# Four-fold streaming of the mixing products, and a mode-major layout of their input

## The chip, the cores and the metric

The kernel runs on one core of a Trainium2 chip. The metric is the device time of one execution in microseconds (us), lower is better. The core has five engines that run at the same time and meet through semaphores: TensorE (PE: matmuls, and PEld, its weight loads), VectorE (DVE), ScalarE (ACT), GpSimd (POOL) and SyncE (SP). SP and POOL issue DMAs here. Matmuls write to PSUM, which has eight banks of 512 float32 columns; ACT and DVE copy results from there to SBUF, the on-chip memory of 128 partitions.

## What is computed

Two operations in a row, on x of shape (8, 5696, 128) and h of shape (5696, 128):

```python
Yf = rfft(x, n=2*S, axis=1) * rfft(h, n=2*S, axis=0)
u0 = irfft(Yf, n=2*S, axis=1)[:, :S, :]          # long convolution

X = rfft(u0, axis=1)                             # 64 lowest modes are mixed
Yr = einsum('bmd,mde->bme', Xr, w_r) - einsum('bmd,mde->bme', Xi, w_i)
Yi = einsum('bmd,mde->bme', Xr, w_i) + einsum('bmd,mde->bme', Xi, w_r)
y = irfft(Yr + 1j*Yi, n=S, axis=1)
u = u0 + y
out = u + relu(u @ w_ch)
```

The mixing is the part that the change touches: for each of 64 modes m, two 128 x 128 weight matrices act on the real and imaginary parts of 8 batches, that is on 16 columns of 128 numbers.

## The kernel before, in words

All transforms are matmuls with constant matrices; operands in SBUF are float16, sums in PSUM float32. A recorder (class Recorder, lines 21 to 121) takes the instructions in the order in which the Python code issues them, keeps that order on each engine, and puts in the waits that the reads and writes of tiles and banks ask for. Nothing is reordered by a scheduler: the program order of each engine is the order of the code.

The batches go in four pairs (g_ = 0 to 3). For each pair, `a_tile` (line 462) makes a first transform (PE products F,Xin; copies to As by ACT and DVE), and `tick` (line 667) runs through the frequencies in steps: `second` (line 608, products As,M), `products` (line 628, the DVE multiplies by the filter, tiles Xs, U and Hs), the first part of the way back (products U,Wc, copies to Zs or Zt, DMA to the scratch tensor zscr), and at line 727 the products G,Zs, which add up the lowest modes of the pair in bank 7 (`MB`). Some matmuls (`keep`, line 575; WARM, line 433) compute nothing that is used.

At the end of each pair two copies bring the modes from bank 7 to the tile XT: line 757 (real and imaginary parts, 256 elements a partition, ACT) and line 759 (the negated imaginary part, 128 elements, ACT; for the last pair the DVE). Copies by two different engines from one bank go one after the other. XT holds 8 x 192 float16 a partition (`XTW` = 192 a batch): before, a batch is a row, with 64 values of -Xi, 64 of Xr and 64 of Xi.

After the last pair comes the stretch that the change is about, in this order on PE (lines 834 to 855):
- `u_z(0, 0, 0, True)`: sixteen products S4a,ZT0a and S4b,ZT0b of 89 columns for the first output tile;
- `mix(0, 16)`, eight more S4 products, `mix(16, 32)`, eight more, `mix(32, 64)`, eight more. `mix` issues for each mode two products with a weight load each (W as weights, XT as the moving operand, 16 columns), adding up in bank 6 (modes 0 to 31) or bank 7 (modes 32 to 63);
- copies of bank 6 (ACT, line 841) and bank 7 (DVE) to the tile Y; then eight transposes of Y by PE (line 846), eight S4 products, and copies of the transposed banks to the tile C (line 851: ACT for the first, DVE for the second half); the DVE then mirrors the second half of the table IBs (`reflect`, line 853).

Then comes the output loop (lines 910 to 928). `u_tile` (line 809) adds to each S4 sum the product of C with the table IBs (`u_c`, line 802, 356 columns) and copies the sum to UT (ACT or DVE); `o_tile` (line 863) multiplies UT by w_ch (products WI,UT), applies relu on ACT (line 893), adds on the DVE (line 894) and writes out by DMA from SP. The S4 products read ZT0 to ZT4, which SP loads from zscr (`load_zt`, line 527): ZT0 to ZT3 before and ZT4 right after the last pair, and each again when its turn is over. The sums take turns in four places of two banks each (`LSLOT`, line 777), so a place must have been copied to UT before PE fills it again.

The part of the code before that issues the products:

```python
for ri, first_col in ((0, M + m), (1, m)):
    mm(pv(6 + m // 32, m % 32 * 2 * B, [[1, 2 * B]]), w_sb[:, (ri * M + m) * D:(ri * M + m + 1) * D],
       bass.AP(xt, first_col, [[B * XTW, P], [M, 2], [XTW, B]]), ri == 0, ri == 1, WT + XTT, [bank(6 + m // 32)])
```

An access pattern is written as pairs of a step and a count: the 16 columns here are two parts (step 64) of eight batches (step 192).

## Time and profile before

| | |
|---|---|
| median of three runs | 379.84 us (379.36 to 381.79) |
| the profiled execution, time | 378.84 us |
| the profiled execution, span from first to last instruction | 377.0 us |
| mean granted clock of TensorE | 0.99 |
| mixing products (XT,W) | 128, from 256.6 to 261.0 us |
| copies to XT on ACT, 256 elements | 4, 386 ns each |
| copies to XT on ACT, 128 elements | 3, 273 ns each |
| copy to XT on the DVE, 128 elements | 1, 290 ns |
| copies to Y | ACT 586 ns, DVE 692 ns |
| products C with IBs, 356 columns | 128, from 263.4 to 363.7 us |

How to read the profile: "busy" is time in which an engine has an instruction in hand; for PE, matmuls overlap, so a busy PE may still stream few columns. In the row of 40 slices a digit is a share in tenths, 9 being 90% or more; PEclk is the share of TensorE's full clock that was granted. A line of a group or of the timeline names the source line, the engine, the operation, the tile written <- tiles read, the shape and the count; in brackets stand the idle time before it and what ended it. The chain that ended last is followed back from the last instruction: each piece is a start, a duration, an engine and a line, and "issue" is time without a visible cause. The times of one profiled execution hold for that execution; each engine's clock time is counted from the start of its span.

### The profile page before, as it was taken

How to read it: one execution, taken by the hardware profiler on the slowest of the kernel's cores; microseconds unless marked ns; L12 is line 12 of the kernel's file. 1: busy time of each engine (PE TensorE's matmuls, PEld its weight loads, DVE VectorE, ACT ScalarE, POOL GpSimd, SP SyncE). 2: the span in 40 equal slices, each digit the busy share in tenths (PEclk: the TensorE clock that was granted, in tenths of full speed). 3: DMA queues.
4: the chain of work that ended last, by engine and by line, in shares of the span. 5: the costliest groups of instructions: out<-in, count | busy, mean ns of one | idle time of the engine just before them, and what ended most of it. 6: DMA issues, size and time to landing. Idle time of an engine off the chain costs nothing.

```text
span 377.0 us, 12488 instructions
## 1 busy us (share of the span) xinstructions
PE 359.5 (95%) x5370; PEld 279.1 (74%) x5370; DVE 294.8 (78%) x336; ACT 314.1 (83%) x495; POOL 75.0 (20%) x117
## 2 busy tenths in 40 slices
PE   7889899999999999999999999999999999999994
PEld 7878766666866666866667766668899889988873
DVE  3649889988998999989998988873437767756666
ACT  8469789998989997999997999995457776788885
POOL 8713011200743220842311301133000000000000
PEclk9999999999999999999999999998899999999999
DMA  7999979979899997999994999999999999999878
GB/s 146 207 285 369 250 163 238 234 201 269 92 148 206 249 246 206 109 137 218 260 269 136 115 345 359 372 358 384 375 394 351 355 416 407 422 408 379 327 292 330
DMA packets 87048, 103.94 MB, mean 276 GB/s; under 512 B 22730, under 2 KB 72522, under 8 KB 83438
## 3 DMA queue, kind: packets, MB, share of 16 engines
q1 hardware_dynamic: 64610, 81.33, 61.4%
q0 software_dynamic: 22384, 21.83, 35.3%
q8 instruction: 42, 0.69, 0.8%
q14 instruction: 12, 0.10, 0.1%
HBM read 70.61 MB, written 51.12 MB: 323 GB/s over the span
## 4 chain that ended last, share of the span: by engine, by line
PE 72%; ACT 10%; DMA 6%; DVE 5%; POOL 3%; issue 3%; DVEq 0%; POOLq 0%
PE ps L323 72%; ACT As L313 7%; DMA Xr<-in_x_dram 4%; DVE As L317 2%; DMA Xt<-in_x_dram 2%; POOL Xr L320 2%; DVE U L622 1%; ACT Zs L311 1%; ACT Xs L311 1%; POOL Hin L320 1%; DVE Xin L365 1%; DVE Hs L315 1%; ACT R L893 1%; ACT Zt L311 1%; DVE U L655 0%
## 5 line engine op out<-in xcount | busy, mean ns | idle before, releaser
L655 DVE TENSOR_TENSOR U<-Xs,Hs 128x2048 f16<-128x2048 f16 (+1 forms) x73 | 86.6, 1192 | 13.9 <-ACT Xs L311 13.0
L323 PE MATMUL ps<-U,Wc 128*128 128x512 f16 (+1 forms) x368 | 94.1, 376 | 1.4 <-DVE U L622 1.4
L311 ACT CAST Xs<-ps 128x1024 f16<-128x1024 f32 (+1 forms) x77 | 74.8, 979 | 10.0 <-PE ps L323 6.9
L311 ACT CAST Zs<-ps 128x512 f16<-128x512 f32 (+1 forms) x132 | 69.2, 594 | 1.7 <-PE ps L323 1.7
L894 DVE TENSOR_TENSOR O<-ps,R 128x512 f32<-128x512 f32 x81 | 52.3, 684 | 20.1 <-ACT R L893 11.2
L317 DVE TENSOR_SCALAR As<-ps 128x720 f16<-128x720 f32 (+1 forms) x67 | 55.6, 880 | 5.7 <-PE ps L323 4.0
L893 ACT ACTIVATE R<-ps 128x512 f32<-128x512 f32 (+1 forms) x92 | 50.5, 591 | 8.5 <-PE ps L323 8.4
L323 PE MATMUL ps<-F,Xin 128*128 128x180 f16 x512 | 52.4, 250 | 3.8 <-DVE Xin L365 2.4
L323 PE MATMUL ps<-As,M 64*128 64x128 f16 (+2 forms) x1488 | 51.9, 215 | 1.2 <-ACT As L313 1.2
L323 PEld LDWEIGHTS ps<-F,Xin 128*128 128x128 f16 x512 | 44.5, 155 | 11.2 <-DVE As L317 3.0
L313 ACT ACTIVATE As<-ps 128x720 f16<-128x720 f32 (+1 forms) x65 | 45.8, 768 | 7.2 <-PE ps L323 6.7
L323 PE MATMUL ps<-WI,UT 128*128 128x256 f16 x360 | 51.0, 278 | 0.5 <-ACT UT L311 0.4
L323 PEld LDWEIGHTS ps<-U,Wc 128*128 128x128 f16 x368 | 28.7, 97 | 30.3 <-ACT Zs L311 3.7
L311 ACT CAST UT<-ps 128x712 f16<-128x712 f32 x46 | 34.5, 752 | 19.5 <-PE ps L323 18.6
L323 PEld LDWEIGHTS ps<-As,M 64*128 64x128 f16 x1488 | 41.6, 94 | 7.5 <-ACT As L313 1.7
L323 PEld LDWEIGHTS ps<-WI,UT 128*128 128x128 f16 x360 | 39.0, 152 | 3.4 <-issue 1.8
L323 PE MATMUL ps<-IBs,C 128*128 128x356 f16 x128 | 40.5, 326 | 0.1
L320 POOL DMA_DIRECT2D Xt<-in_x_dram x40 | 21.5, 541 | 79.1 <-PE ps L323 78.6
L323 PEld LDWEIGHTS ps<-G,Zs 128*128 128x128 f16 x512 | 26.1, 96 | 14.5 <-ACT Zs L311 2.0
L655 DVE TENSOR_TENSOR U<-ps,Hs 128x2048 f16<-128x2048 f32 x15 | 34.2, 2283 | 0.0
L323 PE MATMUL ps<-G,Zs 128*128 128x128 f16 (+2 forms) x512 | 32.3, 192 | 0.1
L311 ACT CAST Zt<-ps 128x512 f16<-128x512 f32 x52 | 28.5, 624 | 0.3 <-PE ps L323 0.3
(74 smaller groups left out, 487.3 us busy)
## 6 DMA issues: line engine op xcount, KB each, us to landing
out_dram<-O SPq DMA_DIRECT2D x39, 512.0 KB, 7.4
zscr<-Zs SPq DMA_DIRECT2D x62, 256.0 KB, 6.3
zscr<-Zt SPq DMA_DIRECT2D x26, 256.0 KB, 6.0
Xt<-in_x_dram POOLq DMA_DIRECT2D x20, 320.0 KB, 6.8
W<-wscr SPq DMA_DIRECT2D x4, 1024.0 KB, 6.7
ZT0a<-zscr SPq DMA_DIRECT2D x4, 1024.0 KB, 7.8
M<-cM POOLq DMA_DIRECT2D x5, 720.0 KB, 17.4
ZT1a<-zscr SPq DMA_DIRECT2D x3, 1024.0 KB, 8.5
```

The costliest lines, as they stand in the source:

```text
L311: R.add(e, lambda h_: h_.copy(dst, src), reads, writes, after=after)
L313: R.add(e, lambda h_: h_.activation(dst, src, COPY, scale=scale), reads, writes, after=after)
L315: R.add(e, lambda h_: h_.tensor_copy(dst, src), reads, writes, after=after)
L317: R.add(e, lambda h_: h_.tensor_scalar_mul(dst, src, scale), reads, writes, after=after)
L320: R.add(eng, lambda h_: h_.dma_start(dst, src), reads, writes, ring=ring, after=after)
L323: R.add("tensor", lambda h_: h_.matmul(o, l, r, start=st, stop=sp), reads, writes)
L365: R.add("vector", lambda e: e.tensor_copy(bass.AP(x_sb, i * XN * XS, [[XW, NQ], [XS, XN], [1, D]]), src), list(toks) + XZ, [("xin", i)])
L622: R.add("vector", lambda e: e.tensor_tensor(bass.AP(u_s[0], b * 512 + d0, [[2048, P], [1024, 2], [D, n], [1, d1 - d0]]), bass.AP(s_[0], s_ ...
L655: R.add("vector", lambda e: e.tensor_tensor(uv, src, hv, MULT), bk + [("h", t, 0), ("h", t, 1, 0), ("h", t, 1, J)], [("u", i)])
L893: R.add("scalar", lambda e: e.activation(rv, src_r, RELU), bk, [("r", i % NR)], after=once(("r", i % NR), G_ALL + XTT + [("y", 0), ("y", 1 ...
L894: R.add("vector", lambda e: e.tensor_tensor(ov, src_u, rv, ADD), bk + [("r", i % NR)], [key + (h_,)], after=once(key, old))
```

## The change

XT gets another layout, and the products another moving operand; nothing else differs.

In XT, 24 neighbours now belong to one mode: 8 of -Xi, 8 of Xr, 8 of Xi, the batches side by side. The copies at lines 757 and 759 write to it in pairs of neighbours (the two batches of a pair) with a step of 24 from mode to mode, and read bank 7 with a step of 128 inside such a pair. Their number, engines and elements are as before.

A product's 16 columns are now neighbours, and its moving operand repeats them n times (a step of 0, n = 4, or fewer for the last three modes of a bank), so that it has 64 columns. The 48 further columns are written to the places of the next three modes in the bank. The first product of a mode starts the sum anew (ri == 0), so the next mode's products overwrite what was put there; the values that stay are those of before.

```diff
-        evac(bass.AP(xt, 2 * g_ * XTW + M, [[B * XTW, P], [XTW, 2], [1, P]]), pv(MB, 0, [[P, 2], [1, P]]),
+        evac(bass.AP(xt, 2 * g_ + B, [[B * XTW, P], [B, 2], [3 * B, M], [1, 2]]), pv(MB, 0, [[M, 2], [1, M], [P, 2]]),
              [bank(MB)], [("xt", g_)], 1.0 / 64, eng="scalar", after=[("ag", k) for k in range(NS + 2 * XN, NK)])
-        evac(bass.AP(xt, 2 * g_ * XTW, [[B * XTW, P], [XTW, 2], [1, M]]), pv(MB, M, [[P, 2], [1, M]]),
+        evac(bass.AP(xt, 2 * g_, [[B * XTW, P], [3 * B, M], [1, 2]]), pv(MB, M, [[1, M], [P, 2]]),
              [bank(MB)], [("xtn", g_)], -1.0 / 64, eng="vector" if g_ + 1 == NP else "scalar", after=[("ag", k) for k in range(NS + 2 * XN, NK)])
...
+    MC = 4
+
     def mix(m0, m1):
         for m in range(m0, m1):
-            for ri, first_col in ((0, M + m), (1, m)):
-                mm(pv(6 + m // 32, m % 32 * 2 * B, [[1, 2 * B]]), w_sb[:, (ri * M + m) * D:(ri * M + m + 1) * D],
-                   bass.AP(xt, first_col, [[B * XTW, P], [M, 2], [XTW, B]]), ri == 0, ri == 1, WT + XTT, [bank(6 + m // 32)])
+            for ri, first_col in ((0, (3 * m + 1) * B), (1, 3 * m * B)):
+                n = min(MC, 32 - m % 32)
+                mm(pv(6 + m // 32, m % 32 * 2 * B, [[1, 2 * B * n]]), w_sb[:, (ri * M + m) * D:(ri * M + m + 1) * D],
+                   bass.AP(xt, first_col, [[B * XTW, P], [0, n], [1, 2 * B]]), ri == 0, ri == 1, WT + XTT, [bank(6 + m // 32)])
```

## The prediction

> **What bounds the kernel now.** I read the page first, then the chain that ended last in order of time, then TensorE's (PE's) granted clock stage by stage, then the instructions around the mixing. Lines of the page:

> ```profile
> span 377.0 us, 12488 instructions
> PE 359.5 (95%) x5370; PEld 279.1 (74%) x5370; DVE 294.8 (78%) x336; ACT 314.1 (83%) x495; POOL 75.0 (20%) x117
> ...
> PEclk9999999999999999999999999998899999999999
> DMA  7999979979899997999994999999999999999878
> ...
> PE 72%; ACT 10%; DMA 6%; DVE 5%; POOL 3%; issue 3%; DVEq 0%; POOLq 0%
> ```

> PE is the bound, and its clock is granted in full except in two of forty slices. The chain, around and behind those slices:

> ```profile
> 262.05 1.05 PE ps L846 x8
> 263.09 90.94 PE ps L323 x1292
> 354.03 0.08 issue
> 354.11 10.27 PE ps L323 x130
> ```

> From 263 to 364 us the end is set by PE alone, matmul behind matmul, with 0.08 us of "issue" between. What PE gains shortly before 263 us should therefore arrive at the end. I then cut the dip into the stretches in which the clock is constant (about 3.41 us each). Columns: busy us and count of each engine, then PEclk, DMA share, GB/s.

> ```profile
> core 0: us, PE busy (x) PEld busy (x) DVE busy (x) ACT busy (x) POOL busy (x), PEclk, DMA share, GB/s
> 24.80:28.21 3.41, 1.68 (x21) 1.44 (x18) 1.77 (x3) 0.47 (x1) 0.90 (x2) 1.00 1.01 387
> 256.91:260.32 3.41, 3.41 (x114) 3.41 (x111) 1.36 (x1) 2.39 (x2) 0.62 (x1) 1.00 1.06 362
> 260.32:263.73 3.41, 3.18 (x56) 2.92 (x53) 1.29 (x3) 0.60 (x1) 0.00 (x0) 0.50 1.05 397
> 263.73:267.15 3.42, 3.42 (x25) 2.33 (x24) 1.49 (x2) 1.41 (x2) 0.00 (x0) 0.50 1.03 356
> ```

> For two stretches, 6.8 us, the clock is exactly half. The stretch ahead of them is full of instructions (PE and weight loads busy 3.41 of 3.41 us), but almost all of these are mixing products. The same stretch, products (tile XT) alone:

> ```profile
> 256.91:260.32 3.41, 3.06 (x98) 2.90 (x95) 0.00 (x0) 0.00 (x0) 1.00 1.06 362
> ```

> The timeline gives the rates (start, us, engine, line, operands, count):

> ```profile
> 256.58 1.11 PE L323 MATMUL ps<-XT,W 128*128 128x16 f16 x32 [0.20 <-issue]
> 257.54 0.20 PE L323 MATMUL ps<-S4a,ZT0a 128*128 128x89 f16 x1
> ...
> 257.87 1.11 PE L323 MATMUL ps<-XT,W 128*128 128x16 f16 x32
> 258.82 0.20 PE L323 MATMUL ps<-S4a,ZT0a 128*128 128x89 f16 x1
> ...
> 259.16 2.05 PE L323 MATMUL ps<-XT,W 128*128 128x16 f16 x64
> 261.05 0.24 PE L323 MATMUL ps<-S4a,ZT0a 128*128 128x89 f16 x1
> ...
> 262.05 1.05 PE L846 MATMUL ps<-Id,Y 128*128 128x128 f16 x8 [0.23 <-issue]
> 262.89 0.28 PE L323 MATMUL ps<-S4a,ZT0a 128*128 128x89 f16 x1
> ...
> 263.49 2.28 PE L323 MATMUL ps<-IBs,C 128*128 128x356 f16 x7
> 265.56 0.28 PE L323 MATMUL ps<-S4a,ZT0a 128*128 128x89 f16 x1
> ...
> 267.25 0.20 PE L323 MATMUL ps<-S4a,ZT1a 128*128 128x89 f16 x1
> ...
> 268.08 0.31 PE L323 MATMUL ps<-IBs,C 128*128 128x356 f16 x1
> 268.24 0.20 PE L323 MATMUL ps<-S4a,ZT1a 128*128 128x89 f16 x1
> ```

> At the full clock a 16-column product takes 29.7 ns (32 from 257.87 to 258.82), an 89-column one 41 ns (8 from 257.54 to 257.87), a 356-column one 160 ns (268.08 to 268.24). In the dip: a 128-column transpose 105 ns (8 from 262.05 to 262.89), 89 columns 75 ns (8 from 262.89 to 263.49), 356 columns 296 ns (7 from 263.49 to 265.56). So the longer forms go at half rate. At 160 ns for 356 columns the array takes 2.2 columns a ns, some 7,600 in 3.41 us. The stretch before the dip streamed 98 x 16 + 16 x 89 = 2,990, or 39% (98 counts a few begun earlier). The stretch at 24.80 us, with the clock kept, has 21 matmuls of 180 columns, some of them begun earlier too, 3,780 columns or 50% at most, though PE was busy in only half of it. What the clock follows, as far as these rows show, is columns streamed and not time occupied.

> **The change part by part.**

> *Products, four times as wide.* The 128 products stay 128, each with its weight load; 116 have 64 columns, the last three of each bank (modes 29 to 31 and 61 to 63, two parts each) 48, 32 and 16. Price at the full clock: no row has 64 columns over all 128 rows of the array, so the ends are the 16-column product (29.7 ns, +0) and an 89-column matmul, 42 ns (sixteen of them and one 356 lie between 267.25 and 268.08: (0.83 - 0.16) / 16), which is +12 ns, or 1.6 us over 128. Between, the line through 89 columns (42 ns) and 356 (160 ns) falls 0.44 ns a column and gives 42 - 25 x 0.44 = 31 ns at 64. I take that, as both its rows are of this kind of stream: +1.3 ns, over 126 +0.16 us, all on the path, as the DVE's copy of Y waits for the last product. [...]

> *Copies into XT with pairs of neighbours.* Same count and elements (ACT 4 of 256 and 3 of 128, DVE one of 128), but written in pairs and read with a stride. No row has this form exactly; the nearest are the As copies (L313, L317), written in pieces of four with a strided source:

> ```profile
> L317 DVE TENSOR_SCALAR As<-ps 128x720 f16<-128x720 f32 x63 | 53.7, 902 | 5.7 <-PE ps L323 4.0
> L313 ACT ACTIVATE As<-ps 128x720 f16<-128x720 f32 x61 | 44.2, 785 | 7.2 <-PE ps L323 6.7
> L313 ACT ACTIVATE XT<-ps 128x256 f16<-128x256 f32 x4 | 1.5, 386 | 1.6 <-PE ps L323 1.6
> L317 DVE TENSOR_SCALAR XT<-ps 128x128 f16<-128x128 f32 x1 | 0.3, 290 | 2.6 <-ACT XT L313 2.6
> ```

> ACT: (785 - 386) / 464 = 0.86 ns an element; DVE: (902 - 290) / 592 = 1.03. Both are one step per element whatever the pieces, so I take 0. Upper end: the element part doubles, 256 x 0.86 + 128 x 1.03 = 0.35 us for the last pair, which lies on the path (PE idles 0.20 us for it at 256.58). At the three earlier group ends the two ACT copies (384 elements) would add 0.33 us each where ACT carries the chain: 1.3 us in all. Below nothing is excluded, since no row shows fewer than one step per element.

> *The dip.* In the stretch before it the products would stream 98 x 64, with the 16 others some 7,700 columns by the same count, the array's whole rate. The stretch after, at full clock, has the last products, sixteen 89s, eight 128s and four 356s, some 29 x 64 + 16 x 89 + 8 x 128 + 4 x 356 = 5,700 columns or 75%, above the 50% that kept its clock. So I take the dip as gone whatever the phase of the stretches. Its worth, replayed from 261.05 us; the other engines around it:

> ```profile
> 261.25 0.69 DVE L315 CAST Y<-ps 128x512 f16<-128x512 f32 x1 [2.99 <-PE ps L323]
> ...
> 262.70 0.60 ACT L313 ACTIVATE C<-ps 128x512 f16<-128x512 f16 x1 [3.09 <-PE ps L846]
> ...
> 263.47 0.93 DVE L549 TENSOR_SCALAR IBs<-IBs,SG 128x2759 f16<-128x2759 f16 x1
> 264.32 0.90 DVE L315 CAST UT<-ps 128x712 f16<-128x712 f32 x1
> 264.92 1.41 ACT L311 CAST UT<-ps 128x712 f16<-128x712 f32 x2 [1.62 <-PE ps L323]
> ```

> - Up to 262.05 nothing is won: the transposes wait for the DVE's Y (0.69 us), not for PE; the eight 89s in between are cover.
> - Transposes 0.84 to 0.42 us, the next eight 89s 0.60 to 0.33: PE done at 262.80 instead of 263.49. But now ACT's C is late: it starts after the fourth transpose (262.05 + 3 x 0.053 + 0.20, the time from start to end of a short matmul at the full clock, = 262.41), ends at 263.01, and PE begins IBs at about 263.10 after 0.3 us of idling. Won 0.39 us.
> - Seven IBs products 2.07 to 7 x 0.16 = 1.12 us: 0.95 won.
> - 265.56 to 267.25 holds eight 89s, a 356, eight 89s, a 356: 1.69 to 0.33 + 0.16 + 0.33 + 0.16 = 0.98; 0.71 won.

> Together 2.05 us; PE would reach its 267.25 at 265.2. The first UT copy must then have freed its bank: DVE's C, reflection (0.93) and copy (0.90), all about 0.4 us earlier, end at 264.8. That holds by 0.4 us.

> *Later.* ZT2 is needed 2 us sooner:

> ```profile
> 255.67 2.09 SPq L320 DMA_DIRECT2D ZT2b<-zscr  x1
> ...
> 271.18 0.20 PE L323 MATMUL ps<-S4a,ZT2a 128*128 128x89 f16 x1
> ```

> ```profile
> ZT2a<-zscr SPq DMA_DIRECT2D x1, 1024.0 KB, 10.1
> ```

> Even with the 10.1 us of the larger part counted from the end of ZT2b's issue (257.76), it lands at 267.9; it would be needed at 269.2. Program order and the number of DMAs on SP's and POOL's queues are unchanged.

> Sum: -2.05 + 0.16 + 0 = -1.9 us. The profiled execution took 378.84 us (span 377.0 and 1.84 outside), 1.00 below the median of the runs, 379.84. So 376.95 for a profile like this one, and 377.9 for the median.

> **Rivals.**

> *The dip stays.* The stretch before it has PE busy 100% and is throttled all the same; if the gate follows something that wider products don't raise, nothing is won and products in the dip become slower: 75/89 = 0.84 ns a column, 54 ns for 64, over the 25 or so products behind 260.32 us (0.73 us at 29.7) + 0.6, and 0.16 as above: 380.6 us. For it: no row shows a 64-column product alone. Against: 24.80 to 28.21, with less occupancy and more columns, kept the clock. [...]

> *The win is given back.* The DMA row shows 9 in nearly every slice of the last third; if transfers set the pace, PE would wait 2 us for ZT loads or for output buffers: 379.8 us. Against: 90.94 us of PE in the chain, and DMA falling to 8 and 7 at the end.

> *Slower: the repeated source streams badly.* The moving operand becomes four repeats of 16 neighbours. If a repeat costs as much as a 16-column product does now (29.7 ns), a product takes 119 ns: 126 x 89 = 11.2 us, less the 2.05: 389 us. It decides from 2.05 / 126 + 29.7 = 46 ns a product. Against: 16 scattered columns take the same 29.7 ns, which looks like a floor per product and not a price per column.

> **How the numbers follow.** Forecast 0.80, dip stays 0.09, given back 0.07, slow source 0.04. The forecast's own range: from the dip's worth with every bit of it PE's (6.8 us at half rate, 3.4 us; a different phase could approach it) 376.4, to 379.4 with products at 42 ns (1.44 more than taken). The runs before spread from 379.36 to 381.79. I give 376.6 to 379.9, which takes in the given-back case and, beside products at 42 ns, copies at 0.35 us. A measurement of this kernel tells about 1% (3.8 us) from no change: faster by that needs 376.0, almost the whole dip's 3.4 us and more, 0.03; slower by that only with the slow source, 0.04; within 1% 0.93.

> **What would show it.** PEclk 1.00 from 256 to 268 us; 32 products in about 1.0 us; transposes 55 ns apart and IBs products 160 ns; the idle time ahead of IBs released by ACT's C; XT copies at 386 and 290 ns; ZT1's first product about 2 us earlier, and every later stage as long as before. Wrong, if the clock still halves, if products take over 46 ns, or if the chain behind 263 us shows a DMA.

## The result, and the profile after

| | before | changed |
|---|---|---|
| median | 379.54 us (14 runs, 378.80 to 381.79) | 378.22 us (14 runs, 377.34 to 379.97) |
| ratio | | 0.9958, 95% interval 0.9942 to 0.9974 |
| profiled execution, span | 377.0 us | 377.3 us |

The change takes 0.42% off, about 1.6 us (1.0 to 2.2), inside the range and in the direction forecast (-1.9 us). The plain difference of the two medians is 1.3 us, inside that interval too. The two profiled spans say the opposite, 377.3 against 377.0 us; this has to be explained first. The page of the changed kernel:

```profile
span 377.3 us, 12488 instructions
...
PEclk9998999999999999999999999999999999999999
```

The dip at slices 28 and 29 is gone, but another stands in slice 4, where the change does nothing. The stretches of the changed kernel, there and at the mixing (columns as before). The clock was 1.00 from 8.25 to 28.73 us, six times 3.413 us, and changed last at 32.15; counted on from there in steps of 3.413 us, stretches begin at 257.43 and 260.84 us here, so the two lines at the mixing begin 0.5 us late; as the clock is 1.00 throughout, they show the same:

```profile
25.32:28.73 3.41, 1.59 (x19) 1.37 (x18) 1.75 (x4) 0.71 (x2) 1.14 (x3) 1.00 1.01 403
28.73:32.15 3.42, 3.42 (x24) 3.42 (x25) 2.42 (x3) 2.51 (x5) 3.02 (x6) 0.50 1.02 423
```

```profile
257.95:261.36 3.41, 3.19 (x104) 3.18 (x103) 1.92 (x2) 2.97 (x2) 1.19 (x1) 1.00 1.09 381
261.36:264.77 3.41, 2.83 (x74) 2.57 (x70) 1.18 (x3) 0.60 (x1) 0.00 (x0) 1.00 1.08 323
```

From there on the changed code is ahead. Its timeline:

```profile
258.21 1.09 PE L323 MATMUL ps<-XT,W 128*128 128x64 f16 x32 [0.22 <-issue]
259.14 0.20 PE L323 MATMUL ps<-S4a,ZT0a 128*128 128x89 f16 x1
...
262.58 0.20 PE L323 MATMUL ps<-S4a,ZT0a 128*128 128x89 f16 x1
...
263.56 0.68 PE L849 MATMUL ps<-Id,Y 128*128 128x128 f16 x8 [0.48 <-issue]
...
264.68 1.24 PE L323 MATMUL ps<-IBs,C 128*128 128x356 f16 x7
...
266.64 0.32 PE L323 MATMUL ps<-IBs,C 128*128 128x356 f16 x1
```

The last line is the ninth product of C with IBs. Before, that one started at 267.06:

```profile
267.06 0.36 PE L323 MATMUL ps<-IBs,C 128*128 128x356 f16 x1
```

Measured from the first mixing product, it comes after 8.43 us (266.64 - 258.21) instead of 10.48 (267.06 - 256.58): 2.05 us won. I use this "local time" below, because it leaves out what happened earlier in an execution. How much of it arrives at the end is read from the time between the ninth and the last (128th) of these products, the "rest": 96.65 us before, 97.27 in this execution. So 0.6 us of the win was lost again here. The chain of this execution:

```profile
264.68 58.35 PE ps L323 x876
323.06 0.63 ACT UT L311
...
328.96 15.85 DMA out_dram<-O
...
345.77 7.48 PE ps L323 x100
```

Where before PE alone made the chain from 263 to 354 us, an output transfer of 15.85 us now stands in it. PE itself idles little for it. Its waits behind the mixing:

```profile
PE ps L323 <- DVE O L897: 0.4, 2, 0.2
PE ps L323 <- ACT UT L311: 0.4, 1, 0.4
```

The first line is 0.20 us at 345.77, right behind the transfer and the DVE's O that waited for it (344.93), and 0.22 us at 354.31, again for the DVE's O, which no transfer precedes in the chain. The second line lies behind the last product of C with IBs. So 0.42 of the 0.6 us are seen as waits, 0.20 of them behind the transfer; the remaining 0.2 us have no visible cause.

### The profile page after: what moved, and what is told of

It is laid out like the page before. It is cut to its first block, busy times and chain, and to the rows that moved or that the text cites. A ratio compares the mean times of both kernels' runs of the same rounds, so it can differ in the third digit from the quotient of the medians.

```text
span 377.3 us, 12488 instructions
## 1 busy us (share of the span) xinstructions
PE 359.0 (95%) x5370; PEld 279.0 (74%) x5370; DVE 295.1 (78%) x336; ACT 314.7 (83%) x495; POOL 75.4 (20%) x117
## 4 chain that ended last, share of the span: by engine, by line
PE 60%; ACT 15%; DMA 9%; DVE 7%; issue 4%; POOL 3%; SPq 1%; DVEq 0%; ACTq 0%; POOLq 0%
PE ps L323 60%; ACT As L313 7%; DMA out_dram<-O 4%; DMA Xr<-in_x_dram 4%; ACT Zs L311 2%; DVE As L317 2%; ACT Xs L311 2%; POOL Xr L320 2%; ACT Zt L311 2%; ACT R L896 1%; DMA Hs<-Hs 1%; DVE Xin L365 1%; POOL Hin L320 1%; DVE U L655 1%; DVE U L622 1%
## 5 line engine op out<-in xcount | busy, mean ns | idle before, releaser
L323 PE MATMUL ps<-U,Wc 128*128 128x512 f16 (+1 forms) x368 | 94.0, 376 | 1.4 <-DVE U L622 1.4
L311 ACT CAST Xs<-ps 128x1024 f16<-128x1024 f32 (+1 forms) x77 | 74.8, 978 | 9.9 <-PE ps L323 6.9
L311 ACT CAST Zs<-ps 128x512 f16<-128x512 f32 (+1 forms) x132 | 69.1, 594 | 1.7 <-PE ps L323 1.7
L317 DVE TENSOR_SCALAR As<-ps 128x720 f16<-128x720 f32 (+1 forms) x67 | 55.8, 881 | 6.7 <-PE ps L323 5.2
L323 PE MATMUL ps<-F,Xin 128*128 128x180 f16 x512 | 53.5, 254 | 3.9 <-DVE Xin L365 2.4
L323 PEld LDWEIGHTS ps<-F,Xin 128*128 128x128 f16 x512 | 45.8, 155 | 11.2 <-DVE As L317 3.3
L323 PE MATMUL ps<-As,M 64*128 64x128 f16 (+2 forms) x1488 | 51.9, 215 | 1.3 <-ACT As L313 1.2
L313 ACT ACTIVATE As<-ps 128x720 f16<-128x720 f32 (+1 forms) x65 | 46.1, 768 | 8.2 <-PE ps L323 7.6
L323 PE MATMUL ps<-WI,UT 128*128 128x256 f16 x360 | 50.9, 278 | 0.5 <-ACT UT L311 0.4
L323 PEld LDWEIGHTS ps<-U,Wc 128*128 128x128 f16 x368 | 28.6, 97 | 30.3 <-ACT Zs L311 3.7
L311 ACT CAST UT<-ps 128x712 f16<-128x712 f32 x46 | 34.5, 752 | 18.2 <-PE ps L323 17.0
L323 PEld LDWEIGHTS ps<-As,M 64*128 64x128 f16 x1488 | 41.6, 94 | 7.6 <-ACT As L313 1.7
L323 PEld LDWEIGHTS ps<-WI,UT 128*128 128x128 f16 x360 | 39.0, 152 | 3.4 <-issue 1.8
L323 PE MATMUL ps<-IBs,C 128*128 128x356 f16 x128 | 39.2, 314 | 0.5 <-DVE O L897 0.4
L320 POOL DMA_DIRECT2D Xt<-in_x_dram x40 | 21.5, 542 | 80.5 <-PE ps L323 80.0
L323 PEld LDWEIGHTS ps<-G,Zs 128*128 128x128 f16 x512 | 26.1, 96 | 14.5 <-ACT Zs L311 2.0
L323 PE MATMUL ps<-G,Zs 128*128 128x128 f16 (+2 forms) x512 | 32.2, 192 | 0.1
L311 ACT CAST Zt<-ps 128x512 f16<-128x512 f32 x52 | 28.5, 622 | 0.2 <-PE ps L323 0.2
## 6 DMA issues: line engine op xcount, KB each, us to landing
W<-wscr SPq DMA_DIRECT2D x4, 1024.0 KB, 7.7
ZT0a<-zscr SPq DMA_DIRECT2D x4, 1024.0 KB, 10.3
ZT1a<-zscr SPq DMA_DIRECT2D x3, 1024.0 KB, 11.0
```

The lines of the kernel that those rows point to most:

```text
L311: R.add(e, lambda h_: h_.copy(dst, src), reads, writes, after=after)
L313: R.add(e, lambda h_: h_.activation(dst, src, COPY, scale=scale), reads, writes, after=after)
L317: R.add(e, lambda h_: h_.tensor_scalar_mul(dst, src, scale), reads, writes, after=after)
L320: R.add(eng, lambda h_: h_.dma_start(dst, src), reads, writes, ring=ring, after=after)
L323: R.add("tensor", lambda h_: h_.matmul(o, l, r, start=st, stop=sp), reads, writes)
```

## The experiments

All ratios are to the kernel before, run alongside on the same chip. The theory (A): the clock follows the columns that PE streams within a stretch of 3.41 us; four-fold streaming keeps that high, and the layout does nothing. The rival (B): the scattered source let the clock fall, and the layout cures it.

**1. The layout alone.**

```diff
-    MC = 4
+    MC = 1
```

> The new layout of XT with products of 16 columns (no repeats). Theory A (the clock follows the columns that PE streams in a stretch of 3.41 us; the layout does nothing): the stretch with most of the products streams some 35 to 40% of what the array can, the clock falls to 0.5 for one or two stretches behind it, first mixing product to ninth product of C with IBs about 10.5 us as before (8.4 us in the changed kernel), time within 0.5 us of the kernel before. Rival B (the scattered source of the products was what let the clock fall): clock 1.00 from 250 to 270 us, 8.5 us, some 1.6 us faster than before.

Measured: ratio 0.9983 (0.9967 to 1.0000), local time 9.88 us. The stretches:

```profile
256.81:260.22 3.41, 3.20 (x113) 3.08 (x110) 2.06 (x2) 3.18 (x2) 1.41 (x1) 1.00 1.03 359
260.22:263.64 3.42, 3.20 (x69) 3.03 (x66) 1.01 (x2) 0.60 (x1) 0.00 (x0) 0.50 1.07 359
263.64:267.05 3.41, 3.41 (x26) 2.23 (x24) 1.77 (x3) 1.41 (x2) 0.00 (x0) 0.50 0.95 348
```

The dip stays in the profiled execution, for two stretches, so B falls as a statement on every execution. But the local time is below 10.5 us, which A did not expect: the products start 25.2 ns apart (the first 32) instead of 29.6. The 29.7 ns that I had taken for a floor per product was not one.

**2. The four-fold streaming alone,** from the old layout.

```diff
-                mm(pv(6 + m // 32, m % 32 * 2 * B, [[1, 2 * B]]), ...
-                   bass.AP(xt, first_col, [[B * XTW, P], [M, 2], [XTW, B]]), ...
+                n = min(4, 32 - m % 32)
+                mm(pv(6 + m // 32, m % 32 * 2 * B, [[1, 2 * B * n]]), ...
+                   bass.AP(xt, first_col, [[B * XTW, P], [0, n], [M, 2], [XTW, B]]), ...
```

> The old layout of XT (source with steps of 64 and 192), but each product's 16 columns streamed four times. Theory A: no dip of the clock around the mixing, first mixing product to ninth product of C with IBs 8.4 to 8.6 us, time as the changed kernel's, about 1.6 us less than before. Rival B (the layout is needed): the dip stays or the products get dearer than 31 ns, so 10 us or more and no gain.

Measured: ratio 1.0253 (1.0231 to 1.0274), 9.6 us slower; local time 19.6 us. Timeline of the products, and stretches:

```profile
257.03 3.68 PE L323 MATMUL ps<-XT,W 128*128 128x64 f16 x32 [0.20 <-issue]
261.11 3.38 PE L323 MATMUL ps<-XT,W 128*128 128x64 f16 x32
264.89 6.97 PE L323 MATMUL ps<-XT,W 128*128 128x64 f16 x64
```

```profile
254.94:258.35 3.41, 3.07 (x44) 2.67 (x42) 1.71 (x2) 2.98 (x5) 2.94 (x4) 1.00 1.10 402
258.35:261.77 3.42, 3.42 (x36) 3.42 (x34) 0.36 (x1) 0.80 (x1) 0.00 (x0) 0.50 1.08 342
```

Theory A's times failed, and with them its clause that the layout does nothing. Rival B's held, in both of its alternatives: the clock is at half for five stretches, from 258.35 to 275.42 us, and the products cost about 110 ns each instead of 29. By the starts in the trace a product of 64 scattered columns takes 110 ns, of 48 84, of 32 57.5: 1.65 ns a column. It takes the same 110 ns before 258.35 us at the full clock and after it at half, so the source is the limit and not the array. At 64 columns in 110 ns a stretch holds 1,984 to 2,376 columns by the starts, and the clock stays at half. Widening needs the neighbours: without them it costs 9.6 us, and the layout without the widening wins 0.6 us, if anything (0.9983, up to 1.0000). In the old pattern each element lay 384 bytes or more from the one read before; in the new one the 16 are neighbours, and 64 columns take 29.0 ns there against 110.

**3. and 4. Twice and eight times.**

```diff
-    MC = 4
+    MC = 2        # and MC = 8
```

> The new layout, columns streamed twice (32 columns a product). Theory A with a limit near 40%, from the stretches seen so far: 89 products of 32 columns and sixteen of 89 in 3.41 us are 52%, so no dip, 8.4 us from first mixing product to ninth product of C with IBs, about 1.6 us less than before, the same as four times. Rival C (the limit for this kind of product lies between half and the whole rate): dip, 10.5 us, no gain.

> The new layout, columns streamed eight times (128 columns a product, fewer for the last seven modes of a bank). No dip by either theory. The price of a product in columns: by a floor of 29 ns and 0.42 to 0.44 ns a column behind it, a product takes 53 to 58 ns, mixing 3.0 to 3.5 us longer than with four times; so about 1.3 to 1.9 us slower than before. If wide products overlap their weight loads better than other rows show (45 ns), about the time of before.

Measured: twice 0.9961 (0.9941 to 0.9981), local time 8.24 us, no dip at the mixing; eight times 1.0055 (1.0037 to 1.0074), 2.1 us slower, local time 11.20 us. Products start 25.2 ns apart at 16 and at 32 columns, 29.0 at 64 and 55.7 at 128. So 25 ns is a floor, and 64 columns are already beyond it. Eight times came out as expected in price (55.7 ns); the mixing became 2.8 us longer than with four times (7.34 us against 4.51), where 3.0 to 3.5 were expected.

Twice, from its page and its timeline:

```profile
PEclk9999999999999999999999999999999999999999
258.20 0.96 PE L323 MATMUL ps<-XT,W 128*128 128x32 f16 x32 [0.21 <-issue]
```

With 4,584 and 4,176 columns in the two stretches at the mixing, 57% and 52% of the 8,090 at full rate, the clock is kept. So C falls, and the limit lies below 52%.

**5. and 6. Filling the early wait,** in the changed kernel and in the kernel before.

```diff
-        for i in range(4 if j < 15 else 26):
+        for i in range(4 if j < 15 else 46):
```

> The changed kernel with 46 in place of 26 idle matmuls (180 columns, result unused) ahead of the first transform of x, so that PE streams through its wait of 1.7 us near 25 us. Theory D (the profiled changed kernel is 1.2 us late from 28.7 us on because a stretch near 25 us streamed 37% of its columns and the clock fell, which depends on where the stretches happen to lie): no dip at 28 us in any phase, time 0.3 to 1.2 us less than the changed kernel's, 2 to 2.8 us less than before, and a smaller spread. Rival (the lag came from loads and the dip was a companion): the same time as the changed kernel, 1.6 us less than before.

> The kernel before with the same 20 further idle matmuls near 25 us. Theory D: the early dip goes where it was there; 0 to 0.6 us less than before in the median, the dip behind the mixing stays (about 10.5 us from first mixing product to ninth product of C with IBs). Against the changed kernel with the same filling the difference is then the change alone: 1.4 to 2.1 us.

Measured: 0.9957 (0.9937 to 0.9977) and 0.9983 (0.9965 to 1.0000). The filled changed kernel shows no early dip, and its median moves by nothing that can be told from the changed kernel's 0.9958; its spread, 2.8 us, is no smaller than the changed kernel's 2.6. Theory D falls as a statement on the median: the early dip may have made one profile late, but taking it away wins nothing that was measured. Nor does the early dip account for the late arrival at the mixing: the kernel of experiment 3 had none and began its mixing at 258.20 us. The filled kernel before keeps its dip of two stretches (259.87 to 266.69 us), with a local time of 9.99 us where 10.5 was expected. Between the two filled kernels the difference is 0.9957 / 0.9983 = 0.9974, 1.0 us with some 1.0 either way, below the 1.4 to 2.1 us expected, though the interval still holds them.

**7. and 8. Half of the output's bytes not written.**

```diff
-            dst = bass.AP(out.tensor, ..., [[NW * D, P], [1, w_]])
-            src = ob[:, 0:w_]
+            dst = bass.AP(out.tensor, ..., [[NW * D, P], [1, w_ // 2]])
+            src = ob[:, 0:w_ // 2]
```

> The kernel before, with each output DMA of whole rows cut to the first half of its bytes; the other half of the output is not written. It is the base for the next run, and shows by itself what the output transfers cost: if they set part of the pace of the last 110 us, 0.5 to 1.5 us less than before; if not, within 0.4 us, but for the last transfer, which ends some 0.3 us sooner.

> The changed kernel with half of the output's bytes not written. Theory E (2.05 us are won behind the mixing and 0.6 of it is given back between 320 and 360 us, where output buffers wait for their transfers): the win against the kernel before with the same cut is 1.9 to 2.1 us, and the lead at the ninth product of C with IBs still stands at the last one. Rival (it is given back to ACT or DVE, or is the spread of one execution): the win against it is about 1.6 us or less and the lead shrinks as it did.

Measured: 0.9968 (0.9947 to 0.9989) and 0.9903 (0.9879 to 0.9926). The 1.2 us that the kernel before gains lie in the range of the first expectation (0.5 to 1.5), but the profile puts them at the very end: from the start of the last product of C with IBs to the end of the span it took 12.03 us, against 13.34 with the whole output. The rest from ninth to last product is 96.62 us in both kernels, hardly less than the 96.65 of the kernel before; with the whole output it lay between 96.64 and 97.34 us in eleven profiles. The lead of the ninth product is kept to the last (1.53 and 1.52 us), as E says. But experiments 10 and 11 keep it with the whole output too, and the longest rest, 97.34 us, is that of experiment 1, with no transfer in its chain and 0.59 us of idling at 325.47 us for which the profile shows no cause. So it is not shown that the transfers take a win back as a rule; what is shown is one transfer in the chain of one execution. The win between the two is 0.9903 / 0.9968 = 0.9935, 2.5 us, with some 1.2 us either way (the two intervals added as squares), too wide to tell 2.05 from 1.6. In the kernel before with half the output, the local time was only 9.55 us (8.37 in the changed kernel with half the output, so 1.2 us won), with a dip of one stretch:

```profile
259.27:262.68 3.41, 3.41 (x108) 3.28 (x104) 0.39 (x2) 1.13 (x2) 0.00 (x0) 1.00 1.09 357
262.68:266.10 3.42, 2.93 (x22) 2.23 (x22) 2.23 (x4) 0.64 (x2) 0.00 (x0) 0.50 0.96 359
```

Here the stretch with the products ended 0.3 us behind the last of them (262.36 and 262.68 us), so that the next one held the longer forms alone, 3,516 columns even at half the clock; and the clock came back one stretch later. So the local time here went with where the stretches lay: 9.55 us with one at half, 9.99 to 10.48 in the three profiles of the old products with two.

**9. Together:** three-fold streaming, and the S4 products that stood between the mixing products put behind them.

```diff
-    for n in range(2):
-        mix(16 * n, 16 * n + 16)
-        u_z(0, 0, 1, True, (n,))
-    mix(32, M)
+    mix(0, M)                    # MC = 3
+    u_z(0, 0, 1, True)
     u_z(0, 1, 0, True, (0,))
```

> The new layout with the columns streamed three times (48), all 128 products in one go, and the sixteen S4 products that stood between them put behind the last product, ahead of the eight that were there. Theory A with a floor: 48 contiguous columns take the 25 ns of a 16- or 32-column product and not the 29 ns of 64, 0.46 us less; the mixing ends 0.66 us earlier and the 0.48 us in which PE waits for Y are filled with work; no dip, as 48 columns each 25 ns are about 80% of the array's rate. First mixing product to ninth product of C with IBs 7.5 us against 8.4 in the changed kernel, time 0.5 to 1.0 us less than the changed kernel's, 2.1 to 2.8 us less than before. Rival: the stretches behind the mixing now hold more waiting and the clock falls again, 9 us or more.

Measured: 0.9951 (0.9933 to 0.9969), median 377.27 us, local time 7.71 us. Timeline:

```profile
257.28 3.37 PE L323 MATMUL ps<-XT,W 128*128 128x48 f16 x128 [0.22 <-issue]
260.51 0.20 PE L323 MATMUL ps<-S4a,ZT0a 128*128 128x89 f16 x1
...
261.53 0.68 PE L847 MATMUL ps<-Id,Y 128*128 128x128 f16 x8
...
262.65 1.24 PE L323 MATMUL ps<-IBs,C 128*128 128x356 f16 x7
...
264.91 0.20 PE L323 MATMUL ps<-S4a,ZT0a 128*128 128x89 f16 x1 [0.28 <-issue]
```

The transposes now follow without idling (0.48 us before), and products take 25 ns. Of the forecast 0.9 us less locally, 0.7 came; the last line shows 0.28 us of idling for which the profile shows no cause. In the time of the whole kernel, 0.9951 against the changed kernel's 0.9958, 1.9 us where 2.1 to 2.8 were expected, the runs can't tell it from the changed kernel. It is the best of the versions by its local time only.

**10. and 11. Both kernels once more,** unchanged.

> The kernel before, unchanged, for one more profile. Theory F (the dip's worth depends on where the stretches of 3.41 us lie against the mixing): it lasts one or two stretches, and first mixing product to ninth product of C with IBs lies anywhere between 9.5 and 10.5 us. Rival (the worth is fixed, and all of the difference to the forecast is given back later): 10.4 to 10.5 us again.

> The changed kernel, unchanged, for one more profile. Theory F: no dip, 8.4 us again from first mixing product to ninth product of C with IBs; from there to the last such product 96.6 us where the output's transfers happen to keep up, up to 97.3 where not.

Measured: local times 10.35 and 8.38 us; rest 96.96 us in both; spans 378.5 and 376.2 us. The kernel before again has two stretches at half:

```profile
257.88:261.30 3.42, 3.38 (x107) 3.41 (x108) 1.72 (x1) 2.75 (x2) 0.98 (x1) 1.00 1.06 387
261.30:264.71 3.41, 3.18 (x66) 3.01 (x63) 0.95 (x2) 0.60 (x1) 0.00 (x0) 0.50 1.09 381
264.71:268.12 3.41, 3.41 (x26) 2.23 (x24) 1.83 (x3) 1.41 (x2) 0.00 (x0) 0.50 0.97 352
```

This pair differs by 1.97 us locally and gives nothing back. Theory F is half borne out: the range 9.5 to 10.5 us appears over the four profiles with the old products (10.48, 10.35, and 9.99 and 9.55 in experiments 6 and 7), but the kernel itself was near its upper end both times.

The other runs bear on this too, as the mean clock of each is on record. A stretch at half takes 3.41 x 0.5 / 378 = 0.0045 off the mean, two take 0.009; the end of an execution, where PE idles, takes up to 0.004 (in experiment 9). Of the 62 runs of the kernel before that stand beside the experiments, 25 had a mean clock of 0.992 or 0.993, which leaves no room for two whole stretches; none had 0.996 or more, which would leave no room for one. The median of the 25 is 378.89 us, that of the other 37 is 379.67, and on each of the three chips the 25 are the faster ones, by 0.3 to 1.1 us. So the dip behind the mixing was often shorter than in the two profiles of this kernel. With the layout alone, two of twelve runs had 0.996 and 1.000: there it can be missing altogether. Of the changed kernel's 14 runs ten had 0.996 or more, median 377.94 us; the other four, the profiled one with its dip in slice 4 among them, 379.10. The clock does not explain every difference: in experiment 5 all nine runs had 0.996 or more, and their times went from 376.82 to 379.66 us.

## Why the prediction was right, step by step

- *What bounds the kernel.* Right: PE carries the chain, and the stretch behind the mixing ran at half clock.
- *The price of the products.* This is the term that was wrong. I expected +1.3 ns a product (+0.16 us); the mixing became 0.10 us shorter (256.58 to 261.05 before, 258.21 to 262.58 after). The rival paragraph called 29.7 ns "a floor per product and not a price per column". Experiments 1 and 2 show the opposite: the same 16 columns as neighbours cost 25 ns, and more scattered columns cost 1.65 ns each, so the old price came from the scattered source. The rival "the repeated source streams badly" foresaw about the right price (119 ns a product, 389 us), but for the wrong reason: repeats of neighbours cost 29 ns; repeats of the old, scattered source cost 110 ns and 9.6 us.
- *Copies into XT.* Right at 0. Lines of the changed kernel: 

```profile
L313 ACT ACTIVATE XT<-ps 128x256 f16<-128x256 f32 x4 | 1.7, 414 | 1.6 <-PE ps L323 1.6
L317 DVE TENSOR_SCALAR XT<-ps 128x128 f16<-128x128 f32 x1 | 0.3, 292 | 2.6 <-ACT XT L313 2.6
```

  386 became 414 ns and 290 became 292, 0.03 us for the pair on the path.
- *The dip goes.* Right. Counted by matmul starts in the trace, the two stretches at the mixing (257.43 to 260.84 and on to 264.25 us) streamed 6,385 and 5,829 columns, where the one ahead of the dip had 2,896; forecast were 7,700 and 5,700. The forecast's margin was smaller than its text says: by starts the stretch at 24.80 us, which kept its clock, had 3,240 columns, 40% of the full 8,090, and not 50%, next to 36% in the one that lost it. The clock fell to 0.50 behind a stretch without a gap (PE busy 3.41 of 3.41 us) and stayed at 1.00 once the same 128 products were wider.
- *Its worth, 2.05 us replayed.* Together with the products -1.9 was forecast locally, -2.05 and -1.97 were measured in the two pairs, of which 0.10 are the products' and the rest the dip's. This size rests on a dip of two stretches, read from one profile; I allowed for a longer dip, not for a shorter one, though 25 of the 62 other runs of the kernel before leave room for one stretch at most. The waits came where they were put: none won before the transposes (PE idles 0.48 us for Y instead of 0.23), and C late by 0.26 us (eight S4 products from 264.08 take 0.34; IBs begins at 264.68).
- *Arrival at the end.* I took all of it as arriving and gave "the win is given back" 0.07. In the first pair of profiles 0.6 of 2.05 us was given back, 0.20 of it seen as a wait behind an output transfer and 0.22 as a further wait for the DVE, and with it came a sign that I had named for being wrong, a DMA in the chain behind 263 us. In the second pair nothing was given back, and its chain shows no DMA there. The rival described that one execution in part; that it lowers the medians is not shown, as rests as long occur without the win (experiment 1). The interval of the win (1.0 to 2.2 us) also holds 2.0.

Open: how the 0.3 us between the forecast of 1.9 us and the measured 1.6 divide between shorter dips in the kernel before, dips elsewhere in the changed kernel, and waits in the output loop. That the sum comes out this close is in part luck, as the products' term and the typical length of the dip were off in opposite directions.

## What to carry to other kernels

Look at the granted clock stretch by stretch: here a stretch with PE busy for 3.41 of 3.41 us, 3.06 of them on products of 16 columns, was followed by two at a clock of 0.50. If the price of a narrow product does not come from its columns (here 25 ns at 16, at 32 and, in experiment 9, at 48), try more columns up to where it rises: here 32 and 48 cost no more than 16, and with 32, 48 and 64 the clock did not dip at the mixing. That was with neighbours as the source; with the scattered source 64 columns took 110 ns and the clock was 0.50 for five stretches. Price a floor by varying one thing (layout or width) before calling it a floor.
